# Linear-attention block with a gated FFN on one core: phi_q@KV of the last eight tiles in pairs, on single PSUM banks

## The chip, the core and the metric

The kernel runs on one core of a Trainium2 chip. A core has five engines with queues of their own: TensorE (PE in the profile, its weight loads PEld), VectorE (DVE), ScalarE (ACT), GpSimd (POOL) and SyncE (SP), which issues the DMAs here. TensorE writes its results to PSUM, which has eight banks of 512 32-bit values in each of 128 partitions. The metric is the device time of one execution in microseconds; the median of several runs counts, and less is better.

## What is computed

One transformer block on 2048 tokens of 640 features, in two halves:

```python
# first half: linear attention, 32 heads of 20
qkv = layernorm(x) @ wqkv
phi(a) = concat(softmax(a @ w_phi), softmax(-(a @ w_phi)))      # 40 per head
kv  = sum over tokens of phi(k) v ;  z = sum over tokens of phi(k)
h   = x + ((phi(q) @ kv) / (phi(q) @ z + 1e-6)) @ wo
# second half: gated FFN of width 1536
n   = layernorm(h)
out = h + (gelu(n @ w_gate) * (n @ w_up)) @ w_down
```

Inputs and output are bf16; sums are held in 32 bits.

## The kernel before

The tokens are 16 tiles of 128, in four blocks of four tiles. A first phase makes, tile by tile, the normalised and transposed input (LN1T, one buffer per block), k and v, and the sums KV over all tokens. Then come the exponentials of q (Eq, transposed, features in partitions) and the attention of tiles 0 to 2. The stretch that matters here is what follows: the FFN, block after block, with the attention of later tiles woven in.

**Units.** The FFN is a list of units. `gate_up(b, f, a0, a1)` (L610) takes one of 12 slices of 128 FFN features: 5 matmuls with the gate weights and 5 with the up weights over up to 512 tokens, a GELU on ScalarE (L618), and the product of both on VectorE (L621), which gives one GT tile. `down(b, tl, u)` (L623) makes half the features (320) of one token tile from all twelve GT tiles with 12 matmuls; after the second half VectorE adds the residual (L641), 640 wide, into y, and SP stores it. Block 0 is done in two passes of 256 tokens with four down units after each; blocks 1 to 3 are 12 gate_up units of 512 tokens and 8 down units.

**Stages.** The attention of a tile t is a chain of stages:

- `attn_a` (L522): phi(q)@KV, named ab. For s in 0, 1 (softmax of plus and minus) and five feature chunks, two matmuls that use half of TensorE's rows each (64 partitions), one for each half u of the heads: 20 matmuls of 88 columns (L510). Then two copies to SBUF (AB, L518), on ScalarE, of both s for one u: 704 columns each.
- `attn_b`, `attn_b2` (L526, L536): the denominator on GpSimd, its reciprocal on VectorE, weights w on GpSimd.
- `attn_b3` (L547): the weighted values on VectorE (tt and o), and a DMA transpose into oT.
- `attn_c` (L565): the output projection, named po, 10 matmuls of 320 columns.
- `attn_d`, `attn_d2` (L574, L587): the residual add with a running sum on VectorE, the square sum on ScalarE, the rest of the statistics on GpSimd.
- `attn_e` (L604): the second layernorm on ScalarE, and a DMA transpose into LN2T, which gate_up of that tile's block reads.

**Order.** The order of every engine's queue is the order of the program. `weave(units, stages)` (L657) issues, ahead of unit i, the stages whose index is i or less; what is left goes to the next weave. For tiles 8 to 15 the stages of four tiles start at units 0, 2, 5 and 7 of the block before theirs, at the offsets LONG:

```python
LONG = (0, 1, 2, 3, 6, 6, 7, 8)          # a b b2 b3 c d d2 e
for tl in range(4):
    stages += attn_at(4 * b + 4 + tl, (0, 2, 5, 7)[tl], LONG)
weave(gus(b, 0, 512) + downs(b, range(4)), stages)
```

**PSUM.** From L490 on PSUM is a ring of four tiles of two banks each (`gtile`, L100). A gate_up takes one (gate in one bank, up in the other), a tile's ab takes two (one per u, with s in its two banks), po one, and the two down units of a token tile share one. A tile is handed on when the engines that read it are through.

Of the kernel before, what the change touches and what calls it, by code (L numbers as in the profile page):

```python
# [8 lines left out]
BF16 = mybir.dt.bfloat16  # L9
F32 = mybir.dt.float32  # L10
ALU = mybir.AluOpType
ACTF = mybir.ActivationFunctionType
AX = mybir.AxisListType
PSUM = bass.MemoryType.PSUM
# [3 lines left out]
def kernel(  # L18
# [12 lines left out]
    nc = tc.nc  # L31
    P = 128
    S = 2048
    D = 640
    H = 32
# [3 lines left out]
    NB = NT // 4  # L39
    NC = D // P  # L40
    NF = FF // P
    EPS = 1e-5
    HD = D // 2
# [15 lines left out]
    KC = Dh + 2  # L59


    UH = H // 2
# [3 lines left out]
    o_v = out.rearrange("b (p t) d -> p (b t) d", t=NT)  # L66
# [4 lines left out]
    ps_cm = ExitStack()  # L71
    psG = ps_cm.enter_context(tc.tile_pool(name="psG0", bufs=4, space=PSUM, reuse_waits="tile"))
# [4 lines left out]
    x_sb = [const.tile([P, 4, D], BF16, name=f"x_sb{b}") for b in range(NB)]  # L77
    wphi = const.tile([P, NC, Dh], BF16, name="wphi")
    Wo = const.tile([P, NC, D], BF16, name="Wo")
# [12 lines left out]
    def eq(t, c, s):  # L92
        for E, g in zip(Eq, QG):
            if t // 4 * NC + c in g:
                return E[:, g.index(t // 4 * NC + c), s, t % 4 * P:(t % 4 + 1) * P]

    def small(pool, shape, name, bufs=3):
        return pool.tile(shape, F32, name=name, bufs=bufs)

    def gtile(name):  # L100
        return psG.tile([P, 2, 512], F32, name=name, tag="G")
# [49 lines left out]


    mid = ctx.enter_context(tc.tile_pool(name="mid", bufs=1, side="right"))
    LN1T = [mid.tile([P, NC, 512], BF16, name=f"LN1T{b}") for b in range(NB)]
    Wq2 = mid.tile([P, NC, D], BF16, name="Wq2")
    p1_cm = tc.tile_pool(name="p1", bufs=1, reuse_waits="tile")
    p1 = p1_cm.__enter__()
# [277 lines left out]
    for t in range(NT):  # L435
        if t == T3:
            ps_cm.close()
            psG = ps_cm.enter_context(tc.tile_pool(name="psG", bufs=3, space=PSUM, reuse_waits="tile"))
# [48 lines left out]
    ev_cm.__exit__(None, None, None)  # L487
    p1_cm.__exit__(None, None, None)
    ps_cm.close()
    psG = ctx.enter_context(tc.tile_pool(name="psG2", bufs=4, space=PSUM, reuse_waits="tile"))  # L490


    p2 = ctx.enter_context(tc.tile_pool(name="p2", bufs=1, reuse_waits="tile"))
# [1 line left out]
    Wd = p2r.tile([P, NF, D], BF16, name="Wd")  # L495
    nc.sync.dma_start(Wd, B_w_down.rearrange("(c p) n -> p c n", p=P))

    LN2T, st = {}, {}

    def attn_a_mm(t):  # L500

        b = t // 4
        if b not in LN2T:
            LN2T[b] = p2.tile([P, NC, 512], BF16, name="LN2T", bufs=2)
        AB = p2r.tile([P, 2, H, KC], F32, name="AB", bufs=2)
        ab = gtile("ab"), gtile("ab")
        for s in range(2):
            for c in range(NC):
                for u, r in enumerate(HALF):
                    nc.tensor.matmul(ab[u][:, s, 3 * c * KC:(3 * c + 4) * KC], lhsT=eq(t, c, s)[r],  # L510
                                     rhs=KV[r, c, s].rearrange("p h f -> p (h f)"),
                                     start=(c == 0), stop=(c == NC - 1), skip_group_check=True)
        st[t] = AB, ab

    def attn_a_ev(t, dve=0):
        AB, ab = st[t]
        for u in range(2):
            (nc.vector.tensor_copy if u >= 2 - dve else nc.scalar.copy)(  # L518
                AB[:, :, u * UH:(u + 1) * UH].rearrange("p s h f -> p s (h f)"), ab[u][:, :, 0:UH * KC])
        st[t] = AB  # L520

    def attn_a(t, dve=0):  # L522
        attn_a_mm(t)
        attn_a_ev(t, dve)

    def attn_b(t, on_pe=False):  # L526

# [36 lines left out]

    def attn_c(t):  # L565

        po = gtile("po")
        for u in range(2):
            for c in range(NC):
                nc.tensor.matmul(po[:, u, 0:HD], lhsT=st[t][:, c, :], rhs=Wo[:, c, u * HD:(u + 1) * HD],  # L570
                                 start=(c == 0), stop=(c == NC - 1))
        st[t] = po

    def attn_d(t, act=True):  # L574

        ht = x_sb[t // 4][:, t % 4, :]
        h2 = ht.rearrange("p (u f) -> p u f", u=2)
        if not act:
            nc.vector.tensor_tensor(h2, st[t][:, :, 0:HD], h2, ALU.add)
            st[t] = ln_stats(p2, [ht], "2", False)[0]  # L580
            return

        sm = small(p2, [P, 2], "sm", 2)
        nc.vector.scalar_tensor_tensor(h2, st[t][:, :, 0:HD], 1.0, h2, op0=ALU.mult, op1=ALU.add, accum_out=sm[:, 0:1])
        st[t] = sm

    def attn_d2(t):  # L587
        sm = st[t]
        ht = x_sb[t // 4][:, t % 4, :]
        sq = p2.tile([P, D], BF16, name="sq", bufs=1)  # L590
        nc.scalar.activation(sq, ht, ACTF.Square, accum_out=sm[:, 1:2])
        v = small(p2, [P, 3], "v2", 2)
        nc.gpsimd.tensor_scalar(v[:, 0:1], sm[:, 0:1], sm[:, 0:1], -1.0 / (D * D), op0=ALU.mult, op1=ALU.mult)
        nc.gpsimd.tensor_scalar_add(v[:, 0:1], v[:, 0:1], EPS)
        nc.gpsimd.tensor_scalar(v[:, 1:2], sm[:, 1:2], 1.0 / D, v[:, 0:1], op0=ALU.mult, op1=ALU.add)
        rstd = small(p2, [P, 1], "rstd2")
        nc.gpsimd.tensor_tensor(rstd, v[:, 1:2], nhalf[:, 0:1], op=ALU.pow)
        nc.gpsimd.tensor_scalar(v[:, 2:3], sm[:, 0:1], rstd, -1.0 / D, op0=ALU.mult, op1=ALU.mult)  # L598
        st[t] = ht, None, rstd, v[:, 2:3]
# [8 lines left out]
        transpose_to(LN2T[t // 4][:, :, t % 4 * P:(t % 4 + 1) * P], ln, on_pe, on_dve)  # L608

    def gate_up(b, f, a0, a1):  # L610
        gu = gtile("gu")
        n = a1 - a0
        for i, W in ((0, Wg), (1, Wu)):
            for c in range(NC):
                nc.tensor.matmul(gu[:, i, 0:n], lhsT=W[:, c, f * P:(f + 1) * P], rhs=LN2T[b][:, c, a0:a1],  # L615
                                 start=(c == 0), stop=(c == NC - 1))
        g = p2.tile([P, 512], BF16, name="g", bufs=3)
        nc.scalar.activation(g[:, 0:n], gu[:, 0, 0:n], ACTF.Gelu_apprx_tanh)  # L618
        if (b, "g", f) not in st:
            st[b, "g", f] = p2.tile([P, 512], BF16, name="GT", bufs=NF + 2)  # L620
        nc.vector.tensor_tensor(st[b, "g", f][:, a0:a1], gu[:, 1, 0:n], g[:, 0:n], ALU.mult)  # L621

    def down(b, tl, u):  # L623
        if u == 0:
            st["pd"] = gtile("pd"), p2.tile([P, D], BF16, name="y", bufs=4)
        pd, y = st["pd"]
        if u == 1 and b == NB - 1 and tl == 3:
            pd = gtile("pd")
        last = b == NB - 1 and tl == 3

        cuts = [(0, 192), (192, HD)] if last and u == 1 else [(0, HD)]
        for n0, n1 in cuts:
            if n0:
                pd = gtile("pd")
            for f in range(NF):
                nc.tensor.matmul(pd[:, u, n0:n1], lhsT=st[b, "g", f][:, tl * P:(tl + 1) * P],  # L636
                                 rhs=Wd[:, f, u * HD + n0:u * HD + n1], start=(f == 0), stop=(f == NF - 1))
            if u == 1 or last:
                a = u if last else 0
                r = lambda x: x.rearrange("p (u f) -> p u f", u=2)[:, a:u + 1, n0:n1]  # L640
                nc.vector.tensor_tensor(r(y), pd[:, a:u + 1, n0:n1], r(x_sb[b][:, tl, :]), ALU.add)  # L641
                f0, f1 = a * HD + n0, u * HD + n1
                stores.append((lag, o_v[:, 4 * b + tl, f0:f1], y[:, f0:f1]))
                if b == NB - 1 and tl >= 2:
                    store(lag)

# [10 lines left out]
    def weave(units, stages):  # L657

        stages = sorted(later + stages, key=lambda x: x[0])
        later.clear()  # L660
        for i, (fn, *args) in enumerate(units):
            while stages and stages[0][0] <= i:
                _, g, *a = stages.pop(0)
                g(*a)
            store(1)
            fn(*args)
        later.extend((i - len(units), g, *a) for i, g, *a in stages)

    def gus(b, a0, a1):
        return [(gate_up, b, f, a0, a1) for f in range(NF)]  # L670

    def downs(b, tls):
        return [(down, b, tl, u) for tl in tls for u in range(2)]
# [40 lines left out]
    def attn_at(t, i, offs):  # L714

        fns = (attn_a, attn_b, attn_b2, attn_b3, attn_c, attn_d, attn_d2, attn_e)
        return [(i + o, fn, t) for fn, o in zip(fns, offs) if o >= 0]

    SHORT = (0, 2, 3, 4, 9, 9, 10, 12)
    SHORT2 = (0, 2, 3, 4, 10, 10, 11, 13)  # L720
    LONG = (0, 1, 2, 3, 6, 6, 7, 8)


    weave(gus(0, 0, 256) + downs(0, (0, 1)),
          attn_at(2, 0, (-1, 0, 1, 2, 7, 7, 8, 10)) + attn_at(3, 1, SHORT) + attn_at(4, 6, SHORT2) + attn_at(5, 9, SHORT2) +
          attn_at(6, 13, SHORT2))
    weave(gus(0, 256, 512) + downs(0, (2, 3)), attn_at(7, 0, SHORT))
    for b in range(1, NB):
        stages = []
        if b + 1 < NB:  # L730
            for tl in range(4):
                stages += attn_at(4 * b + 4 + tl, (0, 2, 5, 7)[tl], LONG)
        weave(gus(b, 0, 512) + downs(b, range(4)), stages)
    man_cm.__exit__(None, None, None)


# [28 lines left out]
```

## Time and profile before

| what | us |
|---|---|
| time, median of 3 runs | 279.58 (279.43 to 279.63) |
| span of the profiled execution, first to last instruction | 277.2 |
| median less span: what lies outside the span | 2.4 |
| TensorE busy | 271.6 |
| VectorE busy | 167.3 |
| ScalarE busy | 143.5 |
| GpSimd busy | 94.7 |

The profiled execution has no time of its own beside its span; the row of 2.4 us sets the span against the runs' median. Three stretches can be told apart in it: to 91 us the first phase and the first tiles, to 141 us block 0 of the FFN, and from there blocks 1 to 3. Block 1 begins at 141.4 us with the ab of tile 8.

How to read it: the profile names a group of instructions by line, engine and operation, and by output and inputs (`gu<-LN2T,Wg`). Matmuls overlap one another, so the length that a row gives one (380 ns for 512 columns) is longer than the time from one start to the next. Where a row of the timeline gives a count, such as x10, its length runs from the first start to the last end. The chain of waits follows the work that ended last back to the start; in order of time it gives TensorE's stretches end to end, so that what a stretch takes beyond its matmuls can be read from it. In brackets, or behind the bar in the groups, stands the idle time of the engine before an instruction and what ended it.

### The profile page before, as it was taken

To read this page: it belongs to the slowest core of one execution; us is meant where nothing else is said; L and a number is where in the kernel's file an instruction comes from. 1 tells how busy PE (TensorE), PEld (TensorE's weight loads), DVE (VectorE), ACT (ScalarE), POOL (GpSimd) and SP (SyncE) were. 2 spreads that over 40 slices of the span, in tenths; PEclk is the share of its full clock that TensorE was granted. 3 is DMA by queue.
4 is the path that set the end of the run, shared out by engine and by line. 5 is a ranking of instruction groups with operands and counts; after the bars stand their busy time and mean duration, and the time that the engine had idled before them with its cause. 6 is when DMAs were issued, how large, how long until landed. Compare 5 with 4: busy or idle time off the path is not lost.

```text
span 277.2 us, 5817 instructions
## 1 busy us (share of the span) xinstructions
PE 271.6 (98%) x2337; PEld 172.1 (62%) x2337; DVE 167.3 (60%) x292; ACT 143.5 (52%) x239; POOL 94.7 (34%) x213
## 2 busy tenths in 40 slices
PE   7899999999999999999999999999999999999995
PEld 3677777764555887788754555675455567444574
DVE  6799999899496776675325757322666622233222
ACT  4879998778598755374524364413445440222200
POOL 4348997765202217365301353400226230000000
PEclk9999999999999999999999999999999999999999
DMA  7965732489730021324120213130022413000011
GB/s 204 192 232 112 99 74 47 44 256 393 255 102 0 4 47 36 85 49 77 30 65 2 47 27 63 32 88 33 14 36 25 73 25 95 26 0 0 0 50 47
DMA packets 42235, 21.37 MB, mean 77 GB/s; under 512 B 35040, under 2 KB 40416, under 8 KB 42208
## 3 DMA queue, kind: packets, MB, share of 16 engines
q1 hardware_dynamic: 42208, 21.01, 30.8%
q8 instruction: 18, 0.29, 0.5%
q14 instruction: 9, 0.07, 0.1%
HBM read 10.18 MB, written 2.62 MB: 46 GB/s over the span
## 4 chain that ended last, share of the span: by engine, by line
PE 87%; SPq 3%; DMA 3%; DVE 2%; ACT 2%; issue 1%
PE gu L615 38%; PE pd L636 19%; PE pq L362 8%; PE po L570 8%; PE pk L274 5%; PE pv L274 4%; PE ab L510 3%; PE kvp L340 2%; SPq L186 2%; DMA LN1T<-ln 2%; DVE stats L110 1%; DMA WkT<-in_A_wqkv_dram 1%; ACT E L307 1%; ACT ln L134 1%; PE wa L228 1%
## 5 line engine op out<-in xcount | busy, mean ns | idle before, releaser
L621 DVE TENSOR_TENSOR GT<-gu,g 128x512 bf16<-128x512 f32 (+1 forms) x60 | 34.4, 580 | 54.3 <-ACT g L618 54.1
L618 ACT ACTIVATE g<-gu 128x512 bf16<-128x512 f32 (+1 forms) x60 | 30.7, 512 | 69.3 <-PE gu L615 68.5
L615 PE MATMUL gu<-LN2T,Wg 128*128 128x512 bf16 (+1 forms) x300 | 61.9, 337 | 0.1
L615 PE MATMUL gu<-LN2T,Wu 128*128 128x512 bf16 (+1 forms) x300 | 61.8, 337 | 0.0
L636 PE MATMUL pd<-Wd,GT 128*128 128x320 bf16 (+2 forms) x396 | 53.8, 295 | 0.0
L636 PEld LDWEIGHTS <-GT 128*128 128x128 bf16 x396 | 37.9, 98 | 15.3 <-DVE GT L621 0.9
L615 PEld LDWEIGHTS <-Wu 128*128 128x128 bf16 x300 | 29.3, 98 | 22.6
L615 PEld LDWEIGHTS <-Wg 128*128 128x128 bf16 x300 | 28.3, 98 | 20.8
L274 PEld LDWEIGHTS <-LN1T 128*128 128x128 bf16 x290 | 27.9, 98 | 11.0 <-DMA LN1T<-ln 0.3
L322 POOL TENSOR_TENSOR vt<-vS,rs 128x672 bf16<-128x672 bf16 x22 | 29.1, 1344 | 9.1 <-DVE rs L318 7.4
L641 DVE TENSOR_TENSOR y<-pd,x_sb 128x640 bf16<-128x640 f32 (+3 forms) x18 | 13.5, 749 | 30.2 <-PE pd L636 30.2
L518 ACT COPY AB<-ab 128x704 f32<-128x704 f32 x28 | 19.6, 748 | 19.8 <-PE ab L510 19.6
L551 DVE TENSOR_TENSOR tt<-AB,w 128x1280 bf16<-128x1280 f32 x16 | 23.8, 1486 | 1.0 <-POOL w L544 0.9
L570 PE MATMUL po<-Wo,oT 128*128 128x320 bf16 x160 | 24.3, 299 | 0.0
L274 PE MATMUL pk<-Wk,LN1T 128*128 128x320 bf16 x160 | 24.0, 299 | 0.0
L314 DVE TENSOR_REDUCE sk<-E 128x64 f32<-128x1280 bf16 x16 | 22.9, 1434 | 1.2 <-ACT E L307 1.2
L362 PE MATMUL pq<-LN1T,Wq 128*128 128x512 bf16 x100 | 22.9, 379 | 0.0
L367 ACT ACTIVATE Eq<-pq 128x1024 bf16<-128x1024 f32 (+1 forms) x26 | 19.9, 830 | 2.4 <-PE pq L362 2.4
L307 ACT ACTIVATE E<-pk 128x640 bf16<-128x640 f32 x28 | 18.3, 716 | 4.5 <-PE pk L274 4.3
L570 PEld LDWEIGHTS <-oT 128*128 128x128 bf16 x160 | 15.6, 98 | 7.0 <-ACT oT L148 0.3
L274 PE MATMUL pv<-Wv,LN1T 128*128 128x320 bf16 x130 | 19.8, 299 | 0.2 <-DMA LN1T<-ln 0.2
L134 ACT ACTIVATE ln<-x_sb,v,rstd 128x640 bf16<-128x640 bf16 x14 | 12.9, 919 | 11.3 <-POOL v L598 11.1
(101 smaller groups left out, 268.1 us busy)
## 6 DMA issues: line engine op xcount, KB each, us to landing
out_dram<-y SPq DMA_DIRECT2D x15, 160.0 KB, 1.8
Wg<-in_B_w_gate_dram SPq DMA_DIRECT2D x1, 1920.0 KB, 9.4
Wu<-in_B_w_up_dram SPq DMA_DIRECT2D x1, 1920.0 KB, 15.3
Wd<-in_B_w_down_dram SPq DMA_DIRECT2D x1, 1920.0 KB, 7.9
x_sb<-in_A_x_dram SPq DMA_DIRECT2D x2, 640.0 KB, 5.5
Wo<-in_A_wo_dram SPq DMA_DIRECT2D x1, 800.0 KB, 11.1
x_sb<-in_A_x_dram SPq DMA_DIRECT2D x4, 160.0 KB, 3.1
Wv<-in_A_wqkv_dram SPq DMA_DIRECT2D x2, 320.0 KB, 4.1
```

The lines of the kernel that those rows point to most:

```text
L274: nc.tensor.matmul(ps[:, u, 0:HD], lhsT=lnT(t, c), rhs=W[:, c, u * HD:(u + 1) * HD], start=(c == 0), stop=(c == NC - 1))
L307: nc.scalar.activation(Ek[t][:, s, :].rearrange("p (u f) -> p u f", u=2), pk[:, :, 0:HD], ACTF.Exp, scale=((lnp[t][2], nrstd[t]) if t in C ...
L314: nc.vector.reduce_sum(sk, Ek[t].rearrange("p s (h f) -> p (s h) f", f=Dh), axis=AX.X)
L322: eng.tensor_tensor(vt[:, s], vS[t % 8], rs[:, s * H:(s + 1) * H, None].to_broadcast([P, H, VC]), ALU.mult)
L362: nc.tensor.matmul(pqs[j][:, i, :], lhsT=Wq2[:, kc, c * P:(c + 1) * P], rhs=LN1T[b][:, kc, :], start=(kc == 0), stop=(kc == NC - 1))
L367: nc.scalar.activation(Eq[j][:, :, s, :], pqs[j][:, 0:len(QG[j])], ACTF.Exp, scale=(1.0, -1.0)[s])
L551: nc.vector.tensor_tensor(tt.rearrange("p s (h f) -> p s h f", f=Dh), num, w[:, :, :, None].to_broadcast([P, 2, H, Dh]), ALU.mult)
L570: nc.tensor.matmul(po[:, u, 0:HD], lhsT=st[t][:, c, :], rhs=Wo[:, c, u * HD:(u + 1) * HD], start=(c == 0), stop=(c == NC - 1))
L615: nc.tensor.matmul(gu[:, i, 0:n], lhsT=W[:, c, f * P:(f + 1) * P], rhs=LN2T[b][:, c, a0:a1], start=(c == 0), stop=(c == NC - 1))
L618: nc.scalar.activation(g[:, 0:n], gu[:, 0, 0:n], ACTF.Gelu_apprx_tanh)
L621: nc.vector.tensor_tensor(st[b, "g", f][:, a0:a1], gu[:, 1, 0:n], g[:, 0:n], ALU.mult)
L636: nc.tensor.matmul(pd[:, u, n0:n1], lhsT=st[b, "g", f][:, tl * P:(tl + 1) * P], rhs=Wd[:, f, u * HD + n0:u * HD + n1], start=(f == 0), sto ...
```

## The change

From down unit 12 of block 0's second pass on (the third token tile of the first block), PSUM is eight tiles of one bank. The ab of tiles 8 to 15 is entered in four pairs: tiles 8 and 9 at unit 14 of that pass, 10 and 11 at the start of block 1, 12 and 13 at its unit 18, 14 and 15 at the start of block 2. Each pair issues 40 matmuls back to back into eight banks, then eight copies of 352 columns, four on ScalarE (u = 0) and four on VectorE (u = 1). The other stages of each tile follow at the offsets of a shorter LONG, two units from tile to tile. What used two banks of one tile now uses two tiles: gate and up, the two halves of po (added by two VectorE instructions, whose sums GpSimd adds), and each down unit (its residual is added at once, 320 wide). AB gets four fixed buffers, two of them in the space of LN1T, which is one tile for all blocks with a view per block. Tiles 0 to 7 keep their order.

```diff
-    LN1T = [mid.tile([P, NC, 512], BF16, name=f"LN1T{b}") for b in range(NB)]
+    LN1F = mid.tile([P, NB * NC * 256], F32, name="LN1T")
+    LN1T = [LN1F.bitcast(BF16).rearrange("p (b c n) -> p b c n", b=NB, c=NC)[:, b] for b in range(NB)]
...
+    def split():
+        ps_cm.close()
+        psB.append(ctx.enter_context(tc.tile_pool(name="psB", bufs=8, space=PSUM, reuse_waits="tile")))
+
+    def bank(name):
+        return psB[0].tile([P, 512], F32, name=name, tag="B")
...
+        if psB:
+            ab = [[None] * 2, [None] * 2]
+            for s in range(2):
+                for u in range(2):
+                    ab[u][s] = bank("ab")
...
+    def attn_pair(t):
+
+        for i in (t, t + 1):
+            attn_a_mm(i)
+        for i in (t, t + 1):
+            AB = ABs[i % len(ABs)]
+            for s in range(2):
+                for u, eng in enumerate((nc.scalar.copy, nc.vector.tensor_copy)):
+                    eng(AB[:, s, u * UH:(u + 1) * UH].rearrange("p h f -> p (h f)"), st[i][u][s][:, 0:UH * KC])
+            st[i] = AB
...
+        if psB:
+            for u in range(2):
+                nc.vector.scalar_tensor_tensor(h2[:, u], st[t][u], 1.0, h2[:, u], op0=ALU.mult, op1=ALU.add,
+                                               accum_out=sm[:, 2 * u:2 * u + 1])
...
+        if psB:
+            nc.gpsimd.tensor_tensor(sm[:, 0:1], sm[:, 0:1], sm[:, 2:3], ALU.add)
...
-        gu = gtile("gu")
+        if psB:
+            gu = bank("gu"), bank("gu")
...
+            ps = pd[:, u, 0:HD] if pd else bank("pd")[:, 0:n1 - n0]
...
+            if pd is None:
+                nc.vector.tensor_tensor(y[:, f0:f1], ps, x_sb[b][:, tl, f0:f1], ALU.add)
...
-    LONG = (0, 1, 2, 3, 6, 6, 7, 8)
+    LONG = (0, 1, 2, 5, 5, 6, 7)
+
+    def attn_rest(t, i):
+        return [(i + o, fn, t) for fn, o in zip((attn_b, attn_b2, attn_b3, attn_c, attn_d, attn_d2, attn_e), LONG)]
...
-    weave(gus(0, 256, 512) + downs(0, (2, 3)), attn_at(7, 0, SHORT))
-    for b in range(1, NB):
-        stages = []
-        if b + 1 < NB:
-            for tl in range(4):
-                stages += attn_at(4 * b + 4 + tl, (0, 2, 5, 7)[tl], LONG)
-        weave(gus(b, 0, 512) + downs(b, range(4)), stages)
+    weave(gus(0, 256, 512) + downs(0, (2, 3)),
+          attn_at(7, 0, SHORT) + [(12, split), (14, attn_pair, 8), (16, attn_pair, 10)] + attn_rest(8, 15) +
+          attn_rest(9, 17) + attn_rest(10, 19) + attn_rest(11, 21))
+    weave(gus(1, 0, 512) + downs(1, range(4)),
+          [(18, attn_pair, 12), (20, attn_pair, 14)] + attn_rest(12, 19) + attn_rest(13, 21) + attn_rest(14, 23) +
+          attn_rest(15, 25))
+    for b in (2, 3):
+        weave(gus(b, 0, 512) + downs(b, range(4)), [])
```

More of the change, by code (lines that the diff above doesn't have):

```diff
@@ L489 @@
     ps_cm.close()
-    psG = ctx.enter_context(tc.tile_pool(name="psG2", bufs=4, space=PSUM, reuse_waits="tile"))
+    ps_cm = ExitStack()
+    psG = ps_cm.enter_context(tc.tile_pool(name="psG2", bufs=4, space=PSUM, reuse_waits="tile"))
     p2 = ctx.enter_context(tc.tile_pool(name="p2", bufs=1, reuse_waits="tile"))
@@ L496 @@
     nc.sync.dma_start(Wd, B_w_down.rearrange("(c p) n -> p c n", p=P))
+    ABs = [p2r.tile([P, 2, H, KC], F32, name=f"AB{i}") for i in range(2)]
+    ABs += [LN1F[:, i * 2 * H * KC:(i + 1) * 2 * H * KC].rearrange("p (s h f) -> p s h f", s=2, h=H) for i in range(2)]
     LN2T, st = {}, {}
+    psB = []
+    def split():
[3 more added lines that the diff above has]
+        return psB[0].tile([P, 512], F32, name=name, tag="B")
     def attn_a_mm(t):
@@ L504, in attn_a_mm @@
             LN2T[b] = p2.tile([P, NC, 512], BF16, name="LN2T", bufs=2)
-        AB = p2r.tile([P, 2, H, KC], F32, name="AB", bufs=2)
-        ab = gtile("ab"), gtile("ab")
+        if psB:
[3 more added lines that the diff above has]
+                    ab[u][s] = bank("ab")
+        else:
+            st[t, "ab"] = gtile("ab"), gtile("ab")
+            ab = [[x[:, s] for s in range(2)] for x in st[t, "ab"]]
         for s in range(2):
@@ L509, in attn_a_mm, with attn_a @@
                 for u, r in enumerate(HALF):
-                    nc.tensor.matmul(ab[u][:, s, 3 * c * KC:(3 * c + 4) * KC], lhsT=eq(t, c, s)[r],
+                    nc.tensor.matmul(ab[u][s][:, 3 * c * KC:(3 * c + 4) * KC], lhsT=eq(t, c, s)[r],
                                      rhs=KV[r, c, s].rearrange("p h f -> p (h f)"),
                                      start=(c == 0), stop=(c == NC - 1), skip_group_check=True)
-        st[t] = AB, ab
-    def attn_a_ev(t, dve=0):
-        AB, ab = st[t]
+        st[t] = ab
+    def attn_pair(t):
[7 more added lines that the diff above has]
+            st[i] = AB
+    def attn_a(t, dve=0):
+        attn_a_mm(t)
+        AB, ab = ABs[t % 2], st[t, "ab"]
         for u in range(2):
@@ L520, in attn_a_ev @@
         st[t] = AB
-    def attn_a(t, dve=0):
-        attn_a_mm(t)
-        attn_a_ev(t, dve)
     def attn_b(t, on_pe=False):
@@ L565, in attn_c @@
     def attn_c(t):
-        po = gtile("po")
+        if psB:
+            po = pos = [bank("po")[:, 0:HD] for u in range(2)]
+        else:
+            po = gtile("po")
+            pos = [po[:, u, 0:HD] for u in range(2)]
         for u in range(2):
             for c in range(NC):
-                nc.tensor.matmul(po[:, u, 0:HD], lhsT=st[t][:, c, :], rhs=Wo[:, c, u * HD:(u + 1) * HD],
+                nc.tensor.matmul(pos[u], lhsT=st[t][:, c, :], rhs=Wo[:, c, u * HD:(u + 1) * HD],
                                  start=(c == 0), stop=(c == NC - 1))
@@ L581, in attn_d @@
             return
-        sm = small(p2, [P, 2], "sm", 2)
-        nc.vector.scalar_tensor_tensor(h2, st[t][:, :, 0:HD], 1.0, h2, op0=ALU.mult, op1=ALU.add, accum_out=sm[:, 0:1])
+        sm = small(p2, [P, 3], "sm", 2)
+        if psB:
+            for u in range(2):
+                nc.vector.scalar_tensor_tensor(h2[:, u], st[t][u], 1.0, h2[:, u], op0=ALU.mult, op1=ALU.add,
+                                               accum_out=sm[:, 2 * u:2 * u + 1])
+        else:
+            nc.vector.scalar_tensor_tensor(h2, st[t][:, :, 0:HD], 1.0, h2, op0=ALU.mult, op1=ALU.add,
+                                           accum_out=sm[:, 0:1])
         st[t] = sm
@@ L610, in gate_up @@
     def gate_up(b, f, a0, a1):
-        gu = gtile("gu")
+        if psB:
+            gu = bank("gu"), bank("gu")
+        else:
+            gu = gtile("gu")
+            gu = gu[:, 0], gu[:, 1]
         n = a1 - a0
@@ L614, in gate_up @@
             for c in range(NC):
-                nc.tensor.matmul(gu[:, i, 0:n], lhsT=W[:, c, f * P:(f + 1) * P], rhs=LN2T[b][:, c, a0:a1],
+                nc.tensor.matmul(gu[i][:, 0:n], lhsT=W[:, c, f * P:(f + 1) * P], rhs=LN2T[b][:, c, a0:a1],
                                  start=(c == 0), stop=(c == NC - 1))
         g = p2.tile([P, 512], BF16, name="g", bufs=3)
-        nc.scalar.activation(g[:, 0:n], gu[:, 0, 0:n], ACTF.Gelu_apprx_tanh)
+        nc.scalar.activation(g[:, 0:n], gu[0][:, 0:n], ACTF.Gelu_apprx_tanh)
         if (b, "g", f) not in st:
             st[b, "g", f] = p2.tile([P, 512], BF16, name="GT", bufs=NF + 2)
-        nc.vector.tensor_tensor(st[b, "g", f][:, a0:a1], gu[:, 1, 0:n], g[:, 0:n], ALU.mult)
+        nc.vector.tensor_tensor(st[b, "g", f][:, a0:a1], gu[1][:, 0:n], g[:, 0:n], ALU.mult)
     def down(b, tl, u):
         if u == 0:
-            st["pd"] = gtile("pd"), p2.tile([P, D], BF16, name="y", bufs=4)
+            st["pd"] = None if psB else gtile("pd"), p2.tile([P, D], BF16, name="y", bufs=4)
         pd, y = st["pd"]
-        if u == 1 and b == NB - 1 and tl == 3:
-            pd = gtile("pd")
         last = b == NB - 1 and tl == 3
@@ L632, in down @@
         for n0, n1 in cuts:
-            if n0:
-                pd = gtile("pd")
+            f0, f1 = u * HD + n0, u * HD + n1
+            ps = pd[:, u, 0:HD] if pd else bank("pd")[:, 0:n1 - n0]
             for f in range(NF):
-                nc.tensor.matmul(pd[:, u, n0:n1], lhsT=st[b, "g", f][:, tl * P:(tl + 1) * P],
-                                 rhs=Wd[:, f, u * HD + n0:u * HD + n1], start=(f == 0), stop=(f == NF - 1))
-            if u == 1 or last:
[L639 to L643, printed above, removed]
+                nc.tensor.matmul(ps, lhsT=st[b, "g", f][:, tl * P:(tl + 1) * P],
+                                 rhs=Wd[:, f, f0:f1], start=(f == 0), stop=(f == NF - 1))
+            if pd is None:
+                nc.vector.tensor_tensor(y[:, f0:f1], ps, x_sb[b][:, tl, f0:f1], ALU.add)
+            elif u == 1:
+                r = lambda x: x.rearrange("p (u f) -> p u f", u=2)
+                nc.vector.tensor_tensor(r(y), pd[:, :, 0:HD], r(x_sb[b][:, tl, :]), ALU.add)
+            if u == 1 or last:
+                a = f0 if last else 0
+                stores.append((lag, o_v[:, 4 * b + tl, a:f1], y[:, a:f1]))
                 if b == NB - 1 and tl >= 2:
```

## The prediction

> **What bounds the kernel now.** I read the busy shares and the clock of the page first, then the chain of work that ended last, in order of time, then the timeline around the places that the change touches, and last the groups with their shapes kept apart.
>
> ```profile
> PE 271.6 (98%) x2337; PEld 172.1 (62%) x2337; DVE 167.3 (60%) x292; ACT 143.5 (52%) x239; POOL 94.7 (34%) x213
> ...
> PE   7899999999999999999999999999999999999995
> ...
> PEclk9999999999999999999999999999999999999999
> ...
> PE 87%; SPq 3%; DMA 3%; DVE 2%; ACT 2%; issue 1%
> ```
>
> TensorE is busy in every slice, at full clock throughout, and holds 87% of the chain; from 34 us on the chain is TensorE with hardly a gap. So in the stretch that the change touches (135 to 261 us) only TensorE's own time counts. A faster copy or a shorter wait elsewhere is worth nothing unless TensorE stood still for it. What can be gained is what its stream holds besides matmuls at their stream rate.
>
> The chain in order of time (start, us, what) shows where that is:
>
> ```profile
> 56.48 1.65 PE kvp L340 x80
> ...
> 68.51 2.41 PE kvp L340 x120
> ...
> 146.89 6.58 PE gu L615 x30
> 153.47 0.50 PE ab L510 x20
> 153.97 2.27 PE gu L615 x10
> ...
> 157.59 2.16 PE gu L615 x10
> ...
> 163.87 6.47 PE gu L615 x30
> ...
> 173.86 1.72 PE pd L636 x12
> ...
> 176.94 11.41 PE pd L636 x84
> ```
>
> Ten gate and up matmuls take 2.16 us after a po (157.59) but 2.27 behind an ab (153.97); thirty take 6.47 against 6.58. So each ab leaves 0.11 us behind it, beside its own 0.50: 0.61 us per tile. How much is matmul work? The kvp matmuls are of the same kind, half an array each with 84 moving columns: 40 more of them cost 2.41 - 1.65 = 0.76 us, 0.019 each. An ab matmul has 88 columns, so 20 of them should take 20 x 0.019 x 88/84 = 0.40 us. The rest, 0.61 - 0.40 = **0.21 us, is paid for going into the half-array matmuls and out again**, once per tile.
>
> The second loss is in the last two lines: 84 down matmuls take 11.41, 0.136 each, so 12 should take 1.63, but the first twelve of a block take 1.72 (173.86, and the same at 220.75). The timeline tells why:
>
> ```profile
> 174.53 0.69 DVE L621 TENSOR_TENSOR GT<-gu,g 128x512 bf16<-128x512 f32 x1 [1.72 <-ACT g L618]
> ...
> 175.27 0.10 PEld L636 LDWEIGHTS <-GT 128*128 128x128 bf16 x1 [0.25 <-DVE GT L621]
> ```
>
> The twelfth matmul waits for the product of the block's last gate_up, which ends at 175.22; TensorE goes on 0.05 us later. The waits view counts four such waits: blocks 1, 2 and 3, and a smaller one (0.01) in block 0.
>
> **The change, part by part.** (1) *Pairs.* Tiles 8 to 15 are entered in four pairs instead of eight singles: four brackets of 0.21 us go, the 320 matmuls stay. 4 x 0.21 = **0.83 us less**.
>
> (2) *One bank per tile.* The waits on TensorE's results, before:
>
> ```profile
> 141.40 0.57 PE L510 MATMUL ab<-KV,Eq 64*128 64x88 bf16 x20
> ...
> 141.51 0.82 DVE L641 TENSOR_TENSOR y<-pd,x_sb 128x640 bf16<-128x640 f32 x1 [2.44 <-PE pd L636]
> 141.90 0.76 PEld L615 LDWEIGHTS <-Wg 128*128 128x128 bf16 x5
> 141.90 1.25 PE L615 MATMUL gu<-LN2T,Wg 128*128 128x512 bf16 x5
> 142.00 1.39 ACT L518 COPY AB<-ab 128x704 f32<-128x704 f32 x2 [4.83 <-PE ab L510]
> ...
> 142.99 1.24 PE L615 MATMUL gu<-LN2T,Wu 128*128 128x512 bf16 x5
> ...
> 144.27 0.60 ACT L618 ACTIVATE g<-gu 128x512 bf16<-128x512 f32 x1 [0.88 <-PE gu L615]
> ```
>
> The GELU reads the gate half only, ready at 141.90 + 1.25 = 143.15, yet starts at 144.27, just after the up half ends (144.23): it waits for the whole two-bank tile. With a tile per bank it can start about 1.08 us sooner, ACT being idle 0.88 before it. Then the product waits for the up half alone and ends 0.6 us (the GELU) sooner. That covers the 0.09 us that the twelfth down matmul lacks, in blocks 1, 2 and 3, which all lie after the split: 3 x 0.09 = **0.27 us less**. Nothing is late next there: the product then ends half a microsecond ahead of that matmul. If waits are not kept per bank, this is 0; it can't be more than 0.27.
>
> (3) *New bank waits.* A pair fills all eight banks, so TensorE now meets releases that it had slack for. Two lie close. Let 0 be the pair's first matmul. The pair streams for 80/2 x 0.0199 = 0.79 us, and its second tile's s=1 half begins at 0.59. The last bank there was the preceding down unit's. The y add starts 0.11 after the first ab matmul (141.40, 141.51); a 320-wide one takes 0.49 (row below), so it ends at 0.60, and 0.05 to TensorE makes 0.65: **a stall of 0.05 us in each of four pairs**, with the rest of the pair and the next unit queued behind it. VectorE is free for that add: in the down stretches it idles 2.44 us before each.
>
> ```profile
> L518 ACT COPY AB<-ab 128x704 f32<-128x704 f32 x28 | 19.6, 748 | 19.8 <-PE ab L510 19.6
> ...
> L349 ACT COPY acc<-kvp 128x420 f32<-128x420 f32 x1 | 0.5, 508 | 0.8 <-DVE kvp L348 0.8
> L641 DVE TENSOR_TENSOR y<-pd,x_sb 128x320 bf16<-128x320 f32 x1 | 0.5, 491 | 0.8 <-PE pd L636 0.8
> ```
>
> The other is the unit after the pair, which wants the pair's first bank. That bank is complete after a quarter of the stream, 0.20. Copies now start 0.20 after their stream ends (142.00 against 141.40 + 0.40), so this one starts at 0.40. Its 352 columns take 748 - 352 x (748 - 508)/(704 - 420) = 451 ns; done at 0.85, seen at 0.90. TensorE comes there at 0.05 + 0.79 + 0.10 = 0.94. Hidden by 0.04, if ACT is idle (it was for 4.83 us here) and each copy waits for its own bank alone. The second bank, on VectorE behind the y add, is free near 1.2 and wanted near 2.0.
>
> So (3) costs 0.20 in all. The trace shows no such wait, so I bound it: at least 0 (a wait can't give time back), at most 0.21 per pair, 0.84: in the wait for GT above the weight loads stood idle for 0.25 us, against 0.04 between two of them in the stream (15.3 us over 396 on the page). I take 0.05, since both ends of it are worked out from rows of the same engines.
>
> (4) *At nothing.* Adds per half are 2 x 0.49 instead of 0.82 on VectorE, under down units of 1.63 us each; without that cover, 0.16 per tile. The residual add in two parts (0.2 us more) and one more POOL operation (0.26) lie ahead of LN2T, wanted some 13 us later, after eight down units. VectorE's four copies per pair (about 2.1 us) end before the first gate_up's product is due at 3.2. Then tt (1.49) and o (0.5) follow, so oT is issued 3.6 us before its po, as now (152.50 and 156.07), against a landing of 2.6: 1 us of cover. SP issues the same transposes and stores, moved past stores only; gate_up of block 1 wants tile 7's LN2T, issued at 137.19 and landed near 140, before 143. LN1T as views of one tile: inside each LN1T block, reads and transposes of different tokens already overlap with no more than 0.16 us of wait. Split: down unit 12 takes the slot of gate_up 9, long free.
>
> Sum: -0.83 - 0.27 + 0.20 = **-0.90 us**. The profiled execution spans 277.2; the timed median is 279.58, so 2.4 lie outside the span, at its ends, which the change leaves alone. 277.2 - 0.9 + 2.4 = **278.7 us**.
>
> A rule against the change: the Trainium skill, "TensorE: Matmul & The Clock Gate", section "The cost: per-tile semaphore tail", says that completions which raise a semaphore queue up, 26 ns each. A pair would raise eight in place of four; by that estimate 4 x 4 x 0.026 = 0.42 us comes back and the sum is -0.48. The trace of before has two such matmuls side by side at the end of each ab, and the copy starts 0.03 us behind them (141.40 + 0.57 = 141.97, then 142.00), which does not show the queueing; so my sum leaves it out.
>
> **Rivals.** *B, most of it eaten:* the GELU gain does not come (waits not per bank), and each pair stalls 0.15, late copy and late add together: -0.83 + 0.60 = -0.23, **279.35**. For it: margins of 0.04 and a queue that can't be filled ahead of a late bank. Against: TensorE picked up 0.05 us after a late VectorE (175.22 to 175.27), with no more lost, and B needs the GELU gain to fail as well.
>
> *C, slower, at the first matmul behind each pair:* the copies wait for the whole pair, not for their banks. Then the first copy starts at 0.79 + 0.20 = 0.99, is done at 1.44 and seen at 1.49 instead of 0.89: 0.60 us, four times. -0.83 + 2.40 = +1.57, **281.15**. It decides from a release 0.21 us late on. For it: GELU waits for a whole tile. Against: that tile spans both banks, the new ones don't.
>
> *D, it touches what it should not:* LN1T as one tile makes the first phase wait. If all twelve transposes cost the one wait of 0.16 seen there, +1.9: **280.6**. Against: the overlap inside a block, above.
>
> **Chances.** Forecast 0.64, B 0.20, C 0.11, D 0.05. A run of this kernel can't tell less than 0.2% (0.56 us) from no change; the forecast lies beyond it, B within, C and D on the other side: faster 0.64, same 0.20, slower 0.16. Low end: no stalls, -1.10 and 0.1 for spread, 278.4. High end: B and the bound of (3), no GELU gain, -0.83 + 0.84, with 0.1 for spread 279.7. That holds the forecast and B and leaves 0.16 out.
>
> **What would show it.** Right: in the chain four ab pieces of x40 near 0.9 us; GELU starting before its up matmuls end; a block's first twelve down matmuls at 1.63; clock unchanged; the first 130 us as before. Wrong: a TensorE wait on an ACT copy behind an ab piece (C), ab pieces over 1.0 us or 1.72 still there (B), PE gaps before 70 us (D).

## The result, and the profile after

The changed kernel takes 278.31 us (median of 13 runs, 277.79 to 278.98), the kernel before 279.44 (13 runs, 278.83 to 279.95). The ratio is 0.9963, with a 95% interval of 0.9953 to 0.9974: 1.03 us less, between 0.73 and 1.31. The forecast was 0.90 less and 278.7 us.

The span of the profiled execution hides this: 277.1 us after, 277.2 before. The chain of waits in order of time says why (start, us, what), here of the kernel after:

```profile
91.79 1.25 PE gu L657 x10
...
139.11 0.94 PE ab L528 x40
140.05 3.37 PE pd L676 x24
143.41 0.93 PE ab L528 x40
144.35 8.74 PE gu L657 x40
...
175.79 9.78 PE pd L676 x72
...
222.24 13.04 PE pd L676 x96
...
274.29 0.29 DVE y L679
```

The first gate_up began at 90.88 us before and begins at 91.79 after. All that the change touches ahead of it is how LN1T and AB are allocated, and that has no effect: with LN1T as one tile the first gate_up begins at 90.72 (e6, below), with LN1T and AB both as after the change at 90.67 (e2). From that start to the start of the last residual add it was 183.46 us (90.88 to 274.34) and is 182.50 (91.79 to 274.29): **0.96 us less**. Two executions are left out as slow: one of the kernel before, at 571.88 us and unexplained, and the profiled one of e7, at a granted clock of 0.95, whose kernel was profiled again (e7b). In the other eleven profiles, these two and nine of the experiments, the first gate_up began anywhere from 90.58 to 91.79, whatever was changed, so the sign "the first 130 us as before" holds only within that spread. The experiments are therefore compared by the stretch from the first gate_up to the last add, beside their times. It came out at 183.46 and 183.47 for two kernels that differ in one allocation, where the spans of the kernel before alone ran from 276.8 to 278.6.

In the lines above, four ab pieces of 40 matmuls take 0.93 to 0.94 us; two singles took 2 x 0.50. Forty gate and up matmuls behind one take 8.74, 0.10 over 40 x 0.216 = 8.64, much as behind a single. So two tiles cost 1.04 in place of 2 x 0.61 = 1.22. And 72 and 96 down matmuls take 0.136 each from the first on: the late twelfth matmul of each block is gone.

The timeline of the kernel after, at its first pair:

```profile
139.05 1.00 PE L528 MATMUL ab<-KV,Eq 64*128 64x88 bf16 x40
139.15 0.49 DVE L679 TENSOR_TENSOR y<-pd,x_sb 128x320 bf16<-128x320 f32 x1 [1.14 <-PE pd L676]
139.45 1.52 ACT L541 COPY AB<-ab 128x352 f32<-128x352 f32 x4 [1.38 <-PE ab L528]
139.56 1.81 DVE L541 COPY AB<-ab 128x352 f32<-128x352 f32 x4
...
139.98 3.43 PE L676 MATMUL pd<-Wd,GT 128*128 128x320 bf16 x24
...
144.28 1.25 PE L657 MATMUL gu<-LN2T,Wg 128*128 128x512 bf16 x5
...
145.57 0.60 ACT L660 ACTIVATE g<-gu 128x512 bf16<-128x512 f32 x1 [0.30 <-PE gu L657]
```

ScalarE's first copy starts 0.40 us after the pair does, while the pair's matmuls run on to 1.00: copies wait for their own bank. The GELU starts at 145.57, 0.04 after its gate half is through (144.28 + 1.25) and a microsecond ahead of the up half's end.

### The profile page after: what moved, and what is told of

It is laid out like the page before. It is cut to its first block, busy times and chain, and to the rows that moved or that the text cites. A ratio compares the mean times of both kernels' runs of the same rounds, so it can differ in the third digit from the quotient of the medians.

```text
span 277.1 us, 5913 instructions
## 1 busy us (share of the span) xinstructions
PE 271.7 (98%) x2337; PEld 173.2 (62%) x2337; DVE 176.5 (64%) x337; ACT 138.9 (50%) x239; POOL 97.0 (35%) x221
## 4 chain that ended last, share of the span: by engine, by line
PE 87%; SPq 4%; DMA 3%; DVE 2%; ACT 2%; issue 1%
PE gu L657 38%; PE pd L676 19%; PE pq L363 8%; PE po L600 8%; PE pk L275 5%; PE pv L275 4%; PE ab L528 3%; SPq L187 2%; PE kvp L341 2%; DMA LN1T<-ln 2%; DVE stats L110 1%; DMA WkT<-in_A_wqkv_dram 1%; ACT E L308 1%; ACT ln L134 1%; PE wa L229 1%
## 5 line engine op out<-in xcount | busy, mean ns | idle before, releaser
L679 DVE TENSOR_TENSOR y<-pd,x_sb 128x320 bf16<-128x320 f32 (+2 forms) x29 | 13.9, 480 | 29.0 <-PE pd L676 29.0
L577 DVE TENSOR_TENSOR tt<-AB,w 128x1280 bf16<-128x1280 f32 x12 | 17.9, 1488 | 1.1 <-POOL w L570 0.9
L363 PEld LDWEIGHTS <-Wq 128*128 128x128 bf16 x100 | 9.5, 98 | 10.4 <-issue 0.2
```

The source lines that it names most:

```text
L363: nc.tensor.matmul(pqs[j][:, i, :], lhsT=Wq2[:, kc, c * P:(c + 1) * P], rhs=LN1T[b][:, kc, :], start=(kc == 0), stop=(kc == NC - 1))
L577: nc.vector.tensor_tensor(tt.rearrange("p s (h f) -> p s h f", f=Dh), num, w[:, :, :, None].to_broadcast([P, 2, H, Dh]), ALU.mult)
```

## The experiments

All are timed against the kernel before unless said. "Stretch" is that from the first gate_up to the last add: 183.46 us before, 182.50 after. (The expectations of e7b and e9 count to the start of the last matmul instead, 0.26 us earlier: 182.24 after the change.)

**Pairs taken apart** (e1), one-bank tiles kept; `attn_pair` takes the number of tiles here, which is 1:

```diff
-          attn_at(7, 0, SHORT) + [(12, split), (14, attn_pair, 8), (16, attn_pair, 10)] + attn_rest(8, 15) +
+          attn_at(7, 0, SHORT) + [(12, split)] + [(i + 6, attn_pair, i, 1) for i in (8, 9, 10, 11)] + attn_rest(8, 15) +
...
-          [(18, attn_pair, 12), (20, attn_pair, 14)] + attn_rest(12, 19) + ...
+          [(i + 6, attn_pair, i, 1) for i in (12, 13, 14, 15)] + attn_rest(12, 19) + ...
```

> The changed kernel with its pairs taken apart: one-bank tiles and per-bank copies stay, but the ab of tiles 8 to 15 are eight singles with one unit between them. Theory (each entry into the half-array matmuls and out again costs 0.21 us): eight brackets again, each ab piece 0.50 with 0.11 behind it, no stall inside; what is left of the gain is the GELU's, 0.27, so about 0.7 us above the changed kernel and a ratio to the kernel before near 0.999. Rival (the gain comes from moving the ab matmuls out of the gate_up stretch, or from the finer banks alone): the time stays with the changed kernel, ratio near 0.9965.

Ratio 1.0003 (0.9988 to 1.0019), stretch 183.18: 0.68 above the changed kernel, 0.28 below the kernel before. The chain shows the ab as eight pieces of x20 at 0.50 again, here three of them:

```profile
138.25 0.50 PE ab L528 x20
138.75 1.74 PE pd L676 x12
...
142.72 0.50 PE ab L528 x20
143.21 2.26 PE gu L657 x10
145.48 0.50 PE ab L528 x20
145.98 6.58 PE gu L657 x30
```

Each leaves about 0.11 behind it, on 12 down matmuls (1.74 against 1.63) as on gate and up matmuls (2.26 against 2.16, 6.58 against 6.47). Six of the eight stand in or next to the down units, as the ab do after the change, and two behind the first gate_up of a block; all cost the same. So it is their number and not their place that counts. A pair has a stall inside that singles don't have. From its first matmul to the one behind it a pair takes 0.934 us, a single here 0.498; 20 more matmuls at 0.0196 each (the mean step from start to start in the stream) are 0.392, which leaves 0.044 for the stall, 0.18 for the four. With it four brackets are 0.68 + 0.18 = 0.86, 0.21 each.

**Pairs on the old ring of two-bank tiles** (e2): the kernel before with the new stage lists, LN1T and AB buffers and

```diff
+    def attn_pair(t):
+        attn_a_mm(t)
+        attn_a_mm(t + 1)
+        attn_a_ev(t, 1)
+        attn_a_ev(t + 1, 1)
```

> Pairs alone: the kernel before with the same four pairs at the same places, but on the ring of four two-bank tiles, copies 704 wide, one on ScalarE and one on VectorE per tile. Theory: the brackets go (-0.83), the GELU gain does not come, and the second tile of each pair now meets the two-bank tile of the down unit before it, whose 640-wide add ends at 0.11 + 0.82 = 0.93 after the pair's start and is seen at 0.98, where the matmul wants it at 0.40: a stall of 0.58 in each pair, +2.3; in all +1.5 us, ratio near 1.005. The first copy (0.60 + 0.75 + 0.05 = 1.40) stays hidden behind it. Rival (single banks are not needed for pairs): -0.8 us, ratio near 0.997.

Ratio 1.0041 (1.0026 to 1.0057), stretch 184.90, 1.44 above the kernel before. Its timeline at the first pair:

```profile
137.93 0.60 PE L513 MATMUL ab<-KV,Eq 64*128 64x88 bf16 x21
138.04 0.82 DVE L650 TENSOR_TENSOR y<-pd,x_sb 128x640 bf16<-128x640 f32 x1 [2.36 <-PE pd L645]
...
138.91 0.55 PE L513 MATMUL ab<-KV,Eq 64*128 64x88 bf16 x19 [0.38 <-DVE y L650]
```

After 21 matmuls TensorE stands still until the 640-wide add is through (138.86) and goes on 0.05 later, 0.98 after the pair's start, as expected to the hundredth. Pairs alone lose; they need the single banks and the 320-wide add.

**Up matmuls first** (e3): the GELU's input comes last again.

```diff
-        for i, W in ((0, Wg), (1, Wu)):
+        for i, W in ((1, Wu), (0, Wg)):
```

> The changed kernel with the up matmuls ahead of the gate matmuls in each gate_up, so that the GELU's input is ready only at the unit's end, as it was. Theory: the product of a block's last gate_up ends 0.6 us later again, the twelfth down matmul waits 0.08 to 0.09 us in blocks 1, 2 and 3 (first twelve 1.72 instead of 1.63), +0.25 us on the changed kernel, ratio near 0.997; in the trace the waits for GT are back to four. Rival (the wait went for another reason, the moved stages freeing ScalarE): first twelve down matmuls stay at 1.63 and the time does not move.

Ratio 0.9974 (0.9961 to 0.9988), stretch 182.79, 0.29 above the changed kernel. TensorE waits four times for GT again, as in the kernel before, where the changed kernel has one such wait, in block 0. In block 2 the chain has

```profile
222.19 13.14 PE pd L676 x96
```

where the changed kernel has 13.04. The early GELU is worth the forecast 0.27 within 0.02, and e1, which keeps it, fits that (0.28 below the kernel before).

**Copy engines swapped** (e4):

```diff
-                for u, eng in enumerate((nc.scalar.copy, nc.vector.tensor_copy)):
+                for u, eng in enumerate((nc.vector.tensor_copy, nc.scalar.copy)):
```

> The changed kernel with the two copy engines swapped: the pair's first bank is now copied by VectorE, behind the residual add. Theory: that add ends at 0.60 after the pair's start, the copy at about 1.1, and the unit behind the pair, due at 0.93, starts at 1.15: a stall of 0.2 to 0.25 us behind each pair, +0.9 us on the changed kernel, ratio near 1.000. Rival (the release of the first bank has slack that my timing of it misses, or a late bank is passed over without a stop): no stall, ratio stays near 0.9965.

A miss: ratio 0.9965 (0.9952 to 0.9978), stretch 182.51, no change. The timeline at the first pair, and the copies' lengths from the view by source line (ns, min/median/max):

```profile
138.74 1.00 PE L528 MATMUL ab<-KV,Eq 64*128 64x88 bf16 x40
...
139.18 1.52 ACT L541 COPY AB<-ab 128x352 f32<-128x352 f32 x4 [1.40 <-PE ab L528]
139.26 1.80 DVE L541 COPY AB<-ab 128x352 f32<-128x352 f32 x4
...
139.68 3.43 PE L676 MATMUL pd<-Wd,GT 128*128 128x320 bf16 x24
```

```profile
L541 ACT COPY AB<-ab x8: 452/464/483, 139.2 to 186.7; 128x352 f32<-128x352 f32 x8
L541 DVE COPY AB<-ab x8: 511/513/515, 139.3 to 187.0; 128x352 f32<-128x352 f32 x8
```

The down unit starts at 139.68, 0.05 after ScalarE's first copy ends (139.18 + 0.45) and before VectorE's does (139.26 + 0.51 = 139.77). So it does not take the pair's first bank, which VectorE copies here. It waits for ScalarE's first copy, which here empties the second bank. Banks are not handed out in turn, then: my picture of a ring was wrong, and the test did not make anything late. That they are handed out in the order in which the schedule expects them free fits this run and e7, but no run tests that rule by itself.

**All copies on VectorE** (e7), so that no bank comes early:

```diff
-                for u, eng in enumerate((nc.scalar.copy, nc.vector.tensor_copy)):
+                for u, eng in enumerate((nc.vector.tensor_copy, nc.vector.tensor_copy)):
```

> The changed kernel with all eight copies of a pair on VectorE. Swapping the engines had shown that the unit behind a pair takes whichever bank is due first, not the pair's first one; here no bank is released early. Theory: VectorE's first copy starts at 0.51 after the pair's start, behind the residual add, takes 0.515, is seen at 1.08 where TensorE comes at 0.935: a stall of 0.14 to 0.15 us behind each of four pairs, 0.6 us in all over the changed kernel, ratio near 0.9985. Rival (the release after a pair is not on the path at all): no stall, ratio near 0.9965.

Ratio 0.9985 (0.9968 to 1.0001). The profile is that of e7b, the same kernel:

> The same kernel as the one with all copies on VectorE, once more for its profile at full clock. Theory: each of the four pairs is followed by a first matmul at 0.28 us behind the last ab matmul instead of 0.13, a stall of 0.145, and the stretch from the first gate_up to the last matmul is 182.24 + 0.58 = 182.82 us. Rival: 0.13 there and 182.24 us.

```profile
137.88 1.00 PE L528 MATMUL ab<-KV,Eq 64*128 64x88 bf16 x40
...
138.39 3.53 DVE L541 COPY AB<-ab 128x352 f32<-128x352 f32 x8
...
138.96 2.74 PE L676 MATMUL pd<-Wd,GT 128*128 128x320 bf16 x19
```

Stretch 183.10, 0.60 above the changed kernel. The next unit starts 1.08 us after the pair (139.98 - 139.05 = 0.93 after the change): 0.15, four times. So the release behind a pair is on the path, and the change clears it by little: in the kernel after, ScalarE's copy ends at 139.45 + 0.45 = 139.90, is seen near 139.95, and TensorE is there at 139.98.

**Four tiles at once** (e8), 16 banks' worth through eight:

```diff
-        for i in (t, t + 1):
+        for i in range(t, t + n):
...
-[(12, split), (14, attn_pair, 8), (16, attn_pair, 10)]
+[(12, split), (15, attn_pair, 8, 4)]
...
-[(18, attn_pair, 12), (20, attn_pair, 14)]
+[(19, attn_pair, 12, 4)]
```

> The changed kernel with four tiles entered together instead of two (tiles 8 to 11 at unit 15, 12 to 15 at unit 19): 16 banks' worth of results through eight banks. Theory: two more brackets go (-0.40), but the third and fourth tile wait for copies of the first two, which VectorE ends at 1.03, 1.46, 1.89 and 2.32 after the start; the fourth tile's last half starts near 2.37 and the stream ends near 2.57 instead of 1.63, +0.94 per group, so +1.5 us on the changed kernel in all, ratio near 1.002. Rival (only the number of brackets counts): -0.4 us, ratio near 0.995.

Ratio 1.0029 (1.0013 to 1.0045), stretch 183.87, 1.37 above the changed kernel. In the middle of a group the chain leaves TensorE for VectorE's copies:

```profile
187.50 1.74 DVE AB L541 x4
...
189.27 0.35 PE ab L528 x9
```

The rate of copies takes over as expected. Eight banks hold two tiles; four at once lose here, and three were not tried.

**LN1T as one tile, alone** (e6), on the kernel before:

```diff
-    LN1T = [mid.tile([P, NC, 512], BF16, name=f"LN1T{b}") for b in range(NB)]
+    LN1F = mid.tile([P, NB * NC * 256], F32, name="LN1T")
+    LN1T = [LN1F.bitcast(BF16).rearrange("p (b c n) -> p b c n", b=NB, c=NC)[:, b] for b in range(NB)]
```

> The kernel before with nothing but LN1T made one tile with a view per block. Theory: reads and writes of other bytes do not wait for each other, so no change, ratio within 0.999 to 1.001. Rival D of the prediction: the first phase waits for transposes of other blocks, some 0.16 us each, up to 1.9 us, ratio up to 1.007.

Ratio 0.9993 (0.9976 to 1.0010), stretch 183.47, first gate_up at 90.72. No change; rival D falls.

**Pairs in block 0 too** (e5: tiles 4 and 5, 6 and 7; an offset of -1 leaves `attn_a` out of a tile's stages):

```diff
+          [(5, split), (8, attn_pair, 4), (13, attn_pair, 6)] +
           ... attn_at(4, 6, (-1,) + SHORT2[1:]) + attn_at(5, 9, (-1,) + SHORT2[1:]) + attn_at(6, 13, (-1,) + SHORT2[1:]))
```

> The changed kernel with the split moved to unit 5 of block 0 and tiles 4 to 7 paired as well (4 and 5 at unit 8, 6 and 7 at unit 13). Theory: each bracket less is worth 0.20 us wherever it stands, so 0.40 us under the changed kernel, less 0.03 per pair, ratio to the kernel before near 0.995; in the trace six ab pieces of x40. Rival (in block 0, where units of 256 tokens leave ScalarE and VectorE less room, all eight banks are not free in time): stalls of 0.2 us or more inside or behind the two new pairs, no gain or a loss.

A miss: ratio 1.0050 (1.0032 to 1.0069), stretch 184.82, 2.32 above the changed kernel. The pair of tiles 4 and 5 went through in 0.94 us, but that of 6 and 7:

```profile
112.33 0.35 DVE L566 RECIPROCAL rd<-den 128x32 f32<-128x32 f32 x1 [1.82 <-POOL den L559]
112.61 0.43 DVE L679 TENSOR_TENSOR y<-pd,x_sb 128x320 bf16<-128x320 f32 x1
...
113.09 0.35 PE L528 MATMUL ab<-KV,Eq 64*128 64x88 bf16 x9 [1.47 <-DVE y L679]
```

TensorE waits 1.47 us for the residual add, the add is queued on VectorE behind a reciprocal, and that waits 1.82 for GpSimd. Two down matmuls ahead of the pair waited for GT as well.

**Tiles 6 and 7 alone** (e9), later, at the start of block 0's second pass. The split stands at unit 14 of the first pass, so the whole second pass runs on single banks:

```diff
+          [(14, split), (16, attn_pair, 6)] + attn_at(2, 0, ...) + ...
...
-          attn_at(7, 0, SHORT) + [(12, split), (14, attn_pair, 8), ...
+          attn_at(6, 0, (-1, 1, 2, 3, 7, 7, 8, 10)) + attn_at(7, 0, (-1, 2, 3, 5, 9, 9, 10, 12)) + [(14, attn_pair, 8), ...
```

> The changed kernel with the split two down units' worth earlier (unit 14 of block 0's first pass) and tiles 6 and 7 paired at the start of its second pass, where VectorE has only a residual add in its queue. Theory: one more bracket less its in-pair stall, 0.20 - 0.03 = 0.17 us under the changed kernel, from the first gate_up to the last matmul 182.07 us against 182.24; ratio near 0.996, which a time can't tell from the changed kernel but the trace can. Rival (block 0 has no room for a pair anywhere): waits of 0.2 us or more appear behind it and the stretch is 182.3 us or longer.

A miss again: ratio 1.0015 (1.0002 to 1.0029), stretch 183.65, 1.15 above the changed kernel.

```profile
127.56 1.12 PE L600 MATMUL po<-Wo,oT 128*128 128x320 bf16 x7 [0.97 <-DMA oT<-o]
```

Tile 6's later chain no longer ends before its po: 0.97 us of TensorE waits for the transposed oT, since VectorE finishes the tile's weighted values only at 124.88. The pair itself gains nothing: the wait for a bank inside it is longer here. From its first matmul to the one behind it the pair takes 1.10 us instead of 0.93, which with 0.11 behind it is what two singles cost (2 x 0.61). In both attempts VectorE's queue, behind GpSimd in e5, took back the bracket or more. That the reason is block 0's units, half as long, is argued and not tested. A block 0 that gains was not found; that none exists is not shown.

## Why the prediction was right

It came out nearly by its own steps.

*Brackets.* Forecast 4 x 0.21 = 0.83, measured 0.86 (e1, with the stalls added back). The way to it, a stream rate from another half-array matmul (kvp) and the excess over it, held.

*Early GELU.* Forecast 0.27, measured 0.29 (e3) and 0.28 (e1).

*Bank waits.* Forecast 0.05 in each pair. The add ended 0.59 after the pair's start (139.15 + 0.49 = 139.64), forecast 0.60, and the matmul that waits for it started 0.65 after the pair's start, as forecast. Of the 0.05 by which it is late, 0.044 is left at the pair's end (e1), 0.18 for the four against a forecast of 0.20. The release behind the pair is hidden by 0.03, forecast 0.04; e7 shows what it costs uncovered. One sentence behind that number was wrong: the next unit does not want "the pair's first bank" but the one due first (e4). In the change itself the two are the same, so the sum did not suffer.

*At nothing.* Added VectorE and GpSimd work did not reach TensorE, which has no wait in the stretch from 135 us on beyond those named. e5 and e9 show that the same work does reach it in block 0.

*Sum.* -0.86 - 0.29 + 0.18 = -0.97, with 0.96 less in the stretch, and 1.03 less (0.73 to 1.31) by the times; forecast -0.90. The brackets were had by adding the stalls to what e1 lost, so the sum tests e1 and e3 against the whole, not the split between brackets and stalls; for the split stands what a single takes beyond its matmuls, 0.61 - 0.392 = 0.22. That the median lies 0.39 below 278.7 is partly the base: the kernel before was 279.58 by three runs and 279.44 by thirteen. One reading was off: 2.4 us do not lie outside the span. In the changed kernel's runs the time less the span is 1.8 to 1.9; the rest is that the profiled execution of the kernel before was faster than its median. It takes nothing from the sum, which is 279.58 - 0.90 either way.

*Rivals.* B fell with the early GELU and a stall of 0.04 us in place of 0.15. C fell with the first copy starting 0.40 after the pair's start; e2 shows the like of it where a tile does span what is still being read. D fell with e6.

*The rule weighed against the change.* The Trainium skill, "TensorE: Matmul & The Clock Gate", section "The cost: per-tile semaphore tail", gives 26 ns for each completion in a queue of them; by that estimate -0.48 would have been left. The measured sum leaves no room for that on the path. An effect of that size can be seen beside it: in e4 ScalarE reads the second of two banks that are completed side by side, and starts 0.44 after the pair's start, where it started 0.40 after it on the first (139.18 - 138.74, 139.45 - 139.05). A few hundredths between neighbours agree with the page; they count only where a copy's start is on the path.

## What to carry to other kernels

Where TensorE is the bound, compare each stretch with its stream rate: what it takes beyond that is the whole prize, and entering and leaving a half-array stream (0.21 us here) can be paid once for several. In this program a tile that spans two banks made the reader of the first wait for the writer of the second. Group only as far as the banks reach, and check for each bank that is reused who frees it and what stands in that engine's queue ahead of it.

## What the runs showed of the hardware

Copies start closer together than they last: ScalarE's of 352 columns last 0.45 us and four end in 1.52; VectorE's last 0.51 and eight end in 3.53, 0.43 apart. Estimates that add full lengths come out too long: the prediction put VectorE's four copies of a pair at about 2.1 us, and they end in 1.81. Why the first phase ends at 90.6 us in one execution and 91.8 in another stays open.
